# A two-layer transformer block on one core: all operations put in a new order, with other engines for 40 of them

## The chip, the cores and the metric

One core of a Trainium2 chip runs the whole program in one launch. The metric is the device time of that core in microseconds (us), the median of the runs.

## The reference

The input `x` is 2048 tokens of 512 features in bf16. Four residual blocks follow each other: attention, token MLP, attention, token MLP, with the same weights in both layers.

```python
def _A_ref(x, wqkv, wo):            # H = 32 heads of 16, window W = 256
    qkv = (x @ wqkv).reshape(B, S, 3, H, Dh).transpose(2, 0, 3, 1, 4)
    scores = einsum("bhqd,bhkd->bhqk", q, k) * (Dh ** -0.5)
    mask = (idx[:, None] - idx[None, :] >= 0) & (idx[:, None] - idx[None, :] < W)
    p = softmax(where(mask, scores, -1e9))
    return einsum("bhqk,bhkd->bhqd", p, v) ... @ wo
def _B_ref(x, w1, b1, w2, b2):      # mixes over the 2048 tokens, F = 1792
    u = gelu(einsum("bsd,sf->bdf", layernorm(x), w1) + b1)
    return (einsum("bdf,fs->bds", u, w2) + b2).transpose(0, 2, 1)
x = x + _A_ref(layernorm(x), ...);  x = x + _B_ref(layernorm(x), ...)   # twice
```

## The kernel before

The kernel first describes its work as a graph of 2440 operations, and only then gives every engine its queue. An operation is a short run of instructions on one engine: two matmuls of 512 columns, one eviction, one mask, one transfer. It knows what it reads and writes, and some operations have a second engine that can do them (`alts`). The string `ORDER` (lines 15 to 42), compressed, holds one order of all 2440 operations and for each the engine that is chosen; `begin_order` (line 44) unpacks it and `replay` (line 175) walks through it once. As it goes it hands each operation to its engine's queue and gives its tiles their buffers: the eight PSUM banks, 7 probability tiles, 4 buffers for `w1`, and so on. `emit` (line 196) then works out which semaphores each operation waits for. Every engine runs its queue strictly in order, so the string fixes who stands behind whom on each engine, which buffer is used again after what, and with it when each transfer may start. No time is in the string.

The work of one layer:

- Normalisation: statistics (line 492) and aggregation (494) on VectorE, the power -0.5 on GpSimd (505), the normalised rows on VectorE (512). In the first tokens of each layer TensorE transposes them (570, evicted at 577 or 579), elsewhere a DMA does (563).
- Projections, 128 columns at a time: K, Q and V operations on TensorE through the helper at line 534; evictions of Q at 592 (VectorE) or 594 (ScalarE), of K at 614 or 616, of V at 649 or 651. K is spread into a block-diagonal tile `kbd` by one of three ways: eight DMAs (624), or two instructions on GpSimd or VectorE (both line 629).
- Attention: 76 score blocks a layer, 152 in all, here numbered 1 to 152 in the order in which TensorE meets them; the order of scores is the same in both strings. A score block (710, some with bias matmuls at 721) fills four banks, ScalarE takes two exponentials from them (736), GpSimd masks the result (757), and TensorE forms the weighted sums (774). In the first eight blocks of 64 queries these come as 64 matmuls and 64 weight loads an operation. Behind a group of scores stand, in turn, a transpose (794) and a reciprocal (798) on VectorE, a product (800) on GpSimd or VectorE, a second transpose on VectorE (805), and the output projection W on TensorE with its residual (816).
- Token MLP: a first part U of `w1` is accumulated already during the attention (evicted at 880, 882 or 884), the rest L (895) behind it, then an addition (906) on VectorE and the gelu on ScalarE (910); the second product Y (534) with its residual (936). Y of the first layer runs into the second layer's attention. Weights come by 128 KB transfers on SyncE's queue (830 and 842).

Between two scores the order puts about three dense operations (K, Q, V, W, U or Y, two matmuls each), so that TensorE works while ScalarE takes its exponentials.

Of the kernel before, what the change touches and what calls it, by code (L numbers as in the profile page):

```python
# [14 lines left out]
ORDER = (
    'c-p;IA&l$T6@5<LtlqS5E3foc@=E@aw=!@gw{j(~WMJTxyp>ln2uP~{Z)K250RaI90R{mEUMV0TAi%&NARr*XARr(hARr)MfI&b&KvV^!(trU0z0PDZG'
    'yl)uzq{)8{y&cW{N8={o_p?j=Ia9EYe}!&L?lJXYD57>h99@89fUDLp4X6kUl)BtcN|Bvzq7yl24gnw>EBc;?T`h*e!p}DhuPnGE8AYJ>?NDc-EU{JnQ'
    'J?<nJLSPGG|{)lB7yQMUn<-s^rO^wmT_FllgSHMyo7)=X^gB#doRt=XP6FyItG%ZO?`+R26o09>x<(6iusP_r={V77bOCO-)l(#u(3gZN@4UCbX31K~Y'
    'YpHNRo}@kqenZGLz6@UYz)#yfp|x8T?7wXO>bO%SFNVItfMN6Pd2j$$dw=3p3G-2P&<Y=g}gb4}CuEaQ3KR}^J1i1i*=oI^m0jRpykB*?Pc5`=D#Qkrx'
    'kzUzmb(QTUTJuml~KQvpz;jkIhr$Jx`RI0aYLEzVtR?wHE?mso@FZD*F(R5v1g*<O-UX8#F{M2gO?QUDEZE}IE8FM@zHW~>6t5j=MjnGaE0V$RhT9nXk'  # L20
    'w`-V&VR_!x6GdIuD-|+xMbF=7WV>}-*Cn@r1DLLlM&uo(13?r;ScW=0>-0J#jvpv*nNdV1lL^n-`_H#@x7lotBtPCC<2c?Q_J@^ux3R2^Y38Q0PWSu$z'
    'qdPQV4CI%Kmk-I<1r*VG^eu^wlvLdk`B|9F@=f!fgtoDu+K(Gk_2rL3ry+ts4NJOej|)Jov_ge^1N}Uv;sxJg;lFHr&fjfGRrs|7}GSY+~qlyWqG+eMX'
    '_GBbbUHC3@po1Ivz_<?P|5^7p40uf(rnoS&ce#-Fn+zg{EnthG7&Ak?vL;86i#t7qAr|Bgw!|G0P;GW*CDvwgH}sqSWo`Xe{tNY};%$Wu;!1Wr_$91c5'
    '^ga^e|P7|-}@f*2Ht@>SOr1bXm0l*d@6r_%{s7Yhh%O}GtsqPznIpleOwm&<Iym_S*Yf|DxiLEX38eR6|ibT%#(@6t3yBd`=o=ZBP`F1!G*3?qt~jYP4'
    'kgt)RULyJiWqa>-zYnVdn7<s;fTnJdD$Z{(Xu;Chp;~Fl)dZH(TfvsyQa_WYupjy*|*K)0fR8<2`nt?hN5Tu%UIz_`_C5@s%y#uV_J3$Z(0&Lrr3P!}R'
    'N4Bi5okqQ0Z%Fc9SF2k6Un;oJG=-AMVllVAow6MnO#9$&EWQIcTCLWXj5QiRemRN&0^uvxG6QJ2dZR8$;Hb_sCd+8IlPjoNMHQa^f}eho*+5MD*0Kn2D'
    'XCN{EnQb(vg>ve57%lAkN`Wji?L;UI*5j7Xoju;eeey``u-l@Km}w09XEKtPvKS(@Amt}av|YD?;y8ioF>U4fk62VA90;dM^<EwwlG#y#mi29)sN$}dH'
    'he*+v^7K!uK^?m;HbIy&$e6N0JkU4~}CTpyRf?{qA&{O_y0VnqW4}*=D;L4gq16VmzH<oK5X4gG8XkXX8m`nt}kKCgSgI?a_ENf_fq}91V}?2m#~WZim'
    'CLANG0<@TqH>F@P6wb&R=|>tafAvmF#V0|w3INEOM1U(>ejA!q5J6u<$u;sTsVqpEG++YUV(_KxdpWZ>7_vaETnHl02^)E0zz9-7VMnj(X8D@BtSh5@}'
    'F>6YCNLstdYElFUkNl_sEP;`i@_`YgX6jfr9^ZnoQd@{+$o2~EP<^CFbfa+{E1zD9mk4=HYUkd(c2r}XU!4t?6_K^52$tF5zDyZ+|gia^e_1)ocjG`z>'  # L30
    '@-*>0j~^sFZ`*ON(+ZFUUV|3QhgxaJqwh0j8?DwFl-jawWLw}K5C(;dpcRp6nU?LGPNs!TKm(ou;;%`8i@rb$&6cFYfldV2)f5R)fQJeYrQh!>P&7$yQ'
    'fm9YEAoOMY9Jx%{lh&JY6x6SQzHG5tgrw~fD>e%g<&|If~=0m(ReWIC(zj_jan@TEog%Vn=Qzlv_nEL4`9Yl6k1iw4PD0p7usKmsu!kqI!#hQBQ=V`aw'
    '2rd351J*zA*HF5Y$&Y96_fw4GxjbMpemru~v*_R9%1+wkD>!P}TV?QI&452OB3TA&^lIw88HXo)rCvJx6n#*wV1)_dQiL;3QIUo@0cmD9gH%0W*2F90?'
    '*C7AFb_5n*w3x{XQ5aYqQ$q9Bh56l&;zkfY*>5|ZacV6_mVX58=jy(NlKG>GEy#0G(Kp=X0ut5&UsehZ^EvVtaRG#i#v#kK?TRkbX>@M@TrYT1#BR7nM'
    ';!$ejrCPD*?Vl3)uYViW9uT}z#RCPG}RZjw486rN<^*e#bD@aA4bdG1D7>0PYI2^M5@^BbGOeQllo{WQ>F<SH$%kSZM1ZsqFFP_LyKY*&Af&kN0KJ*PE'
    '3?u3{+x~n$M`(!`i{_+g<~oKZu2wQQj0TM~brQoik!iG>aLBs`)Z8!tHIo`xLb5DM5IOp}_W4_bpMCV<**K1a3;JcoT^4ZXmE742hsx#i*bP_wme1oi*'
    'DcOtW$wBYei|yQ7$}u~YR4k_#|bwVub+sp1paPbq<HiAP`dmPL`wJ^#nS{*y2QYt3nb^fN>_03`IGlL|7vCQ_CvY+VOZt2f#hCzyxv^~xtAl5RjIfXae'
    'd4ni4uCl?N1e%d)}GDPa}^oaKDrs*Erq+;NvlWlmMkSAbX1L0?{*tAL-0}!0>B^k4w%Fa$Na?$*;QN?cU%%3gB;SfB1FFKEHC0!j-;+mA;1g{Qvi;^aA'
    'qIxhlow=KXp+*6XowuR!F^tl?gh_z6?YJyzj58*{H||Ev#>-B~W*UfSt(qurt><tP{b&bKgj_EWwLl;3YjRQ?GHmP({_&bNf#7Nk<?b?#4~6_?VJc3ep'
    'IDSaxwC(n9v{;=e(gZMQH_!*D#HJh7q!CiC#;L`&Bh{Xr(SjKOO#``JbYduOY^DmWN-EgIgdOX#={HYU!<31Frw+F5*{6fusMISs<@}&>%g@#-;g?s<~'  # L40
    'OMQHNd>npS#c|KeUZ(aUo&TXiaL>W~Tn+jtA%8<PdrLX5U|tT`r%#AiHF@vn=LPuxP~iUpKz>0O'
)
# [973 lines left out]
```

## Time and profile before

| what | value |
|---|---|
| runs, median of 3 (lowest to highest) | 447.27 us (446.93 to 448.69) |
| profiled execution, span first to last instruction | 443.6 us |
| median of the runs less the span | 3.67 us |
| granted TensorE clock | 1.000 |
| busy: TensorE / VectorE / ScalarE / GpSimd | 96% / 70% / 72% / 47% |
| transferred | 45.01 MB in 98,736 packets |

The profile gives the profiled execution's time as its span alone; what lies around it (start and end of the launch) is the third row. The busy share of TensorE counts pipelined matmuls whose ends are modelled, so 96% does not say that it runs at its peak; how far apart the matmuls stand tells that. A wait that the profile puts down to "issue" is one that no semaphore, engine or transfer of the profile accounts for.

### The profile page before, as it was taken

To read this page: it belongs to the slowest core of one execution; us is meant where nothing else is said; L and a number is where in the kernel's file an instruction comes from. 1 tells how busy PE (TensorE), PEld (TensorE's weight loads), DVE (VectorE), ACT (ScalarE), POOL (GpSimd) and SP (SyncE) were. 2 spreads that over 40 slices of the span, in tenths; PEclk is the share of its full clock that TensorE was granted. 3 is DMA by queue.
4 is the path that set the end of the run, shared out by engine and by line. 5 is a ranking of instruction groups with operands and counts; after the bars stand their busy time and mean duration, and the time that the engine had idled before them with its cause. 6 is when DMAs were issued, how large, how long until landed. Compare 5 with 4: busy or idle time off the path is not lost.

```text
span 443.6 us, 14593 instructions
## 1 busy us (share of the span) xinstructions
PE 426.4 (96%) x6344; PEld 193.6 (44%) x6344; DVE 308.7 (70%) x573; ACT 317.4 (72%) x362; POOL 207.9 (47%) x316
## 2 busy tenths in 40 slices
PE   7898989999999999999999999999999999999996
PEld 6453444444433444444444444443344444444452
DVE  7997778778896579564787777789988456521134
ACT  3998999999999941726989899999999870440000
POOL 3486445746486531011566687968867751000000
PEclk9999999999999999999999999999999999999999
DMA  8574522301143446632255322131130447763533
GB/s 244 161 127 73 105 66 47 84 16 30 46 106 92 133 117 185 183 89 71 63 100 154 89 40 57 45 94 23 34 93 15 111 125 197 210 182 102 149 94 106
DMA packets 98736, 45.01 MB, mean 101 GB/s; under 512 B 28912, under 2 KB 98672, under 8 KB 98672
## 3 DMA queue, kind: packets, MB, share of 16 engines
q1 hardware_dynamic: 98672, 44.07, 39.1%
q8 instruction: 50, 0.82, 0.8%
q14 instruction: 14, 0.11, 0.1%
HBM read 33.56 MB, written 2.10 MB: 80 GB/s over the span
## 4 chain that ended last, share of the span: by engine, by line
PE 80%; ACT 12%; DVE 6%; issue 1%; POOL 0%; POOLq 0%
PE PS L534 54%; ACT pt L736 12%; PE PS L710 9%; PE PS L895 8%; PE PS L774 8%; DVE kbd L603 1%; DVE stats L492 1%; DVE xh_sb L512 1%; PE PS L721 1%; DVE rl L794 1%; DVE bb L472 0%; DVE qT L592 0%; DVE stg L614 0%; PE PS L570 0%; DVE vst L649 0%
## 5 line engine op out<-in xcount | busy, mean ns | idle before, releaser
L736 ACT ACTIVATE pt<-PS 128x1024 bf16<-128x1024 f32 (+1 forms) x304 | 281.7, 1036 | 16.0 <-PE PS L710 12.2
L757 POOL TENSOR_TENSOR pt<-pt,ldm 128x256 int32<-128x256 int32 (+2 forms) x226 | 145.1, 668 | 81.6 <-ACT pt L736 79.1
L534 PE MATMUL PS<-xh_sb,w1b 128*128 128x512 bf16 x280 | 68.9, 381 | 0.4 <-ACT pt L736 0.2
L534 PE MATMUL PS<-uT,w2b 128*128 128x512 bf16 (+1 forms) x294 | 69.1, 369 | 0.0
L534 PE MATMUL PS<-xhT,wqkv 128*128 128x512 bf16 (+1 forms) x288 | 67.0, 357 | 2.0 <-issue 0.6
L710 PE MATMUL PS<-qT,kbd 32*128 32x256 bf16 (+4 forms) x1488 | 60.2, 251 | 4.3 <-ACT pt L736 2.1
L505 POOL TENSOR_TENSOR rstd<-agg,mhalf 128x2 f32<-128x2 f32 (+1 forms) x33 | 22.8, 693 | 73.3 <-DVE agg L494 73.3
L936 DVE SCALAR_TENSOR_TENSOR x_sb<-PS,b2col,x_sb 128x512 bf16<-128x512 f32 x31 | 22.9, 746 | 46.6 <-PE PS L534 46.5
L794 DVE STREAM_TRANSPOSE rl<-PS 128x1024 f32<-128x1024 f32 x32 | 39.7, 1242 | 13.8 <-PE PS L774 13.3
L710 PEld LDWEIGHTS PS<-qT,kbd 32*128 32x128 bf16 x1488 | 21.6, 92 | 62.5 <-ACT pt L736 43.4
L910 ACT ACTIVATE uT<-rl,b1col 128x512 bf16<-128x512 f32 x28 | 18.5, 713 | 40.1 <-DVE rl L906 40.1
L774 PE MATMUL PS<-pt,vb 64*17 64x320 bf16 (+4 forms) x2976 | 43.5, 252 | 3.8 <-issue 1.9
L492 DVE BATCH_NORM_STATS2 stats<-x_sb 128x6 f32<-128x512 bf16 x64 | 43.1, 682 | 1.0
L534 PE MATMUL PS<-uT,pt 128*128 128x512 bf16 x168 | 41.2, 379 | 0.0
L534 PEld LDWEIGHTS PS<-uT,w2b 128*128 128x128 bf16 x294 | 27.2, 98 | 31.2 <-issue 3.2
L774 PEld LDWEIGHTS PS<-pt,vb 64*17 64x17 bf16 x2976 | 31.2, 84 | 19.1 <-issue 9.2
L534 PEld LDWEIGHTS PS<-xh_sb,w1b 128*128 128x128 bf16 x280 | 23.7, 98 | 31.8 <-issue 6.2
L895 PE MATMUL PS<-xh_sb,w1b 128*128 128x512 bf16 x168 | 37.4, 379 | 0.0
L534 PEld LDWEIGHTS PS<-xhT,wqkv 128*128 128x128 bf16 x288 | 23.9, 97 | 28.9 <-issue 5.5
L534 PE MATMUL PS<-wqkv,xhT 128*128 128x512 bf16 x128 | 33.9, 381 | 0.5 <-ACT pt L736 0.3
L534 PE MATMUL PS<-wo_sb,oT 128*128 128x512 bf16 x128 | 32.5, 380 | 0.2 <-DVE oT L805 0.2
L512 DVE TENSOR_SCALAR xh_sb<-x_sb,agg,rstd 128x512 bf16<-128x512 bf16 x64 | 29.7, 484 | 2.7 <-POOL rstd L505 2.5
(64 smaller groups left out, 339.8 us busy)
## 6 DMA issues: line engine op xcount, KB each, us to landing
w1b<-in_B_w_dram SPq DMA_DIRECT2D x112, 128.0 KB, 2.8
w2b<-in_B_w_dram SPq DMA_DIRECT2D x70, 128.0 KB, 2.8
pt<-in_B_w_dram SPq DMA_DIRECT2D x42, 128.0 KB, 2.8
vb<-vst SPq DMA_DIRECT2D x64, 68.0 KB, 2.1
out_dram<-x_sb SPq DMA_DIRECT2D x15, 128.0 KB, 2.0
x_sb<-in_A_x_dram SPq DMA_DIRECT2D x3, 512.0 KB, 7.5
wqkv<-in_A_wqkv_dram SPq DMA_DIRECT2D x4, 256.0 KB, 3.8
kbd<-stg SPq DMA_DIRECT2D x48, 16.0 KB, 1.9
```

The lines of the kernel that those rows point to most:

```text
L492: op("vector:stat", lambda e: e.bn_stats(st[:, 0:6], x_sb[:, t, :]), reads=[f"x{t}"], writes=[("st", i)], cost=dve_cost(512))
L505: op("gpsimd:rstd", lambda e: e.tensor_tensor(rstd[:, t0:t1, 0], agg[:, t0:t1, 1], mhalf[:, 0:1].to_broadcast([P, t1 - t0]), op=ALU.pow), ...
L512: op("vector:xh", lambda e: e.tensor_scalar(xh_sb[:, t, :], x_sb[:, t, :], agg[:, t, 0:1], rstd[:, t, :], op0=ALU.subtract, op1=ALU.mult), ...
L534: return e.matmul(o, lhsT=w, rhs=x, start=start, stop=stop, skip_group_check=True)
L710: last = e.matmul(bank(tt[r // 2], r % 2)[:, base + c0 * 64:base + (c0 + n) * 64], lhsT=kbd[32 * r:32 * r + 32, tk.slot, o, jj].rearrange( ...
L736: op("scalar:exp", lambda e, ts=ts, tp=tp, i=i, cols=cols: e.activation(probs(tp)[:, i, 0:cols, :], pair(ts)[:, :, 0:cols].rearrange("p r ...
L757: return e.tensor_tensor(v, v, m, op=ALU.mult)
L774: last = e.matmul(bank(t, h)[32 * r:32 * r + 17, i + q0 * 64:i + (q0 + n) * 64], lhsT=vb[64 * h:64 * h + 64, tk.slot, jj, 4 * o + r, :], r ...
L794: op("vector:od", lambda e, t=tod, tr=tr: e.transpose(rl[:, tr.slot:tr.slot + 2].rearrange("p a b -> p (a b)"), pair(t)), reads=[(tod, i) ...
L895: last = e.matmul(bank(tu, tt), lhsT=v()[:, sc - b0, k0 + tt * P:k0 + (tt + 1) * P], rhs=xh_sb[:, sc, :], start=(sc == b0), stop=(sc == NT ...
L910: op("scalar:gelu", lambda e, ft=ft, tt=tt: e.activation(uT[:, ft, :], rl[:, tmps[tt].slot], ACTF.Gelu_apprx_tanh, bias=b1col[:, ft:ft + 1 ...
L936: op("vector:resy", lambda e: e.scalar_tensor_tensor(x_sb[:, t, :], bank(ft), b2col[:, t:t + 1], x_sb[:, t, :], op0=ALU.add, op1=ALU.add), ...
```

## The change

Only the string `ORDER` is replaced. The graph, the operations, the buffers and the code that gives out queues and semaphores stay.

```diff
 ORDER = (
-    'c-p;IA&l$T6@5<LtlqS5E3foc@=E@aw=!@gw{j(~WMJTxyp>ln2uP~{Z)K250RaI90R{mEUMV0TAi%&NARr*XARr(hARr)MfI&b&KvV^!(trU0z0PDZG'
...
+    'c-p;HKZx_l6(4zLzti5$7bY-;K9~!0puiNmpaTUI(18Lf6i^|84jgdd!Urx~xX^(L6)IG?Foy~k3aD_QfD02`nBc;N3kO`daIuApEnIA|#THv^v4x9_*WO+4'
...
 )
```

Unpacked, the two strings compare like this. All five queues differ, most operations by a few places: on average an operation moves 4.6 places of 922 on TensorE, 4.4 on VectorE, 3.1 on ScalarE, 3.3 on GpSimd and 10.3 on SyncE. The sequence of the 152 scores is untouched. Of the operations that may run on either of several engines, 40 change:

| operations | from | to | how many |
|---|---|---|---|
| Q, K, U, V evictions, transposed rows | VectorE | ScalarE | 15 |
| Q, K, V evictions | ScalarE | VectorE | 6 |
| K spread (629, 624) | GpSimd | VectorE | 6 |
| K spread | DMA | VectorE / GpSimd | 2 / 2 |
| product (800) | GpSimd | VectorE | 6 |
| product | VectorE | GpSimd | 2 |
| the ones of `vst` (479) | VectorE | GpSimd | 1 |

Operations on each queue, before and after: TensorE 922 and 922; VectorE 559 and 561; ScalarE 359 and 368; GpSimd 299 and 292; SyncE 301 and 297. K spreads on GpSimd, DMA, VectorE: 13, 6, 5 before and 9, 2, 13 after. Products on GpSimd and VectorE: 18 and 14 before, 14 and 18 after.

TensorE's queue between scores, where it matters here (P is one weighted-sum operation, T a transpose of rows, the number behind a letter how many stand together):

```
behind score   before                          after
 3 ..  6       V4 | Q T2 | Q K | K V2 K        V Q V | V2 T2 | - | K Q K V2 K
13, 14         P2 | V2                         P | V2 P
17, 18         Q3 | Q P2                       Q P Q2 | Q P
37 .. 40       U2 | P2 | U2 | U3               U3 | U P2 | U3 | U3
48, 49         P2 | U2                         P | P
60, 61         U2 W2 | W3                      U2 W2 | W3
76 (to the second layer's first score)
   before   U7 P2 U8 W2 U W6 U7 L26 Y L Y L Y27 T Y2 V2 Y T Y2 V Y V T2 Y3 K2 Y2 Q2 V2
   after    U7 P2 U8 W4 U2 W2 U W U4 W U L22 Y L5 Y3 L Y30 T Y3 T Y2 T2 V Y3 K2 V Q4
77 .. 80       Q2 Y2 | V2 Y2 K | K3 Y2 | Y3    V2 K V | V3 K3 | Y4 | Y3
128, 129       V4 | P2                         V3 | V P2
147 .. 149     U4 | U2 P2 | U3                 U3 | U3 P2 | U3
152 (to the end)
   before   U8 P2 U2 L3 W6 L W2 L31 Y L7 Y118
   after    U7 P2 U L2 U L W8 L39 Y119
```

On VectorE, the operation of line 512 that stood between the K eviction behind the 59th score and the V eviction that follows it is moved behind the next U eviction. On ScalarE, evictions among the exponentials: a Q eviction more behind the 17th score; between the 78th and the 104th score eight where there were five; three U evictions behind the 148th and 150th scores where there were none, and four behind the last score where there were three.

More of the change, by code (lines that the diff above doesn't have):

```diff
@@ L20 @@
[L20 to L24, printed above, removed]
@@ new lines @@
+    'NVc*z7gx)rZQEqE`f@g-o6U?;v>FcifYR~k?(U8nMQON*e0lM;b<<dPEWE%=X9dwLoN9=Vo17!WSnl--R;v{`8+g1d*>cJ3@O|9YvQTV@`f(kFjD=AUgsre$'
+    'mjA9V@Th3F+et!`s7Pp0q!H~kBfshgxY=lUp55>Wvn;<FRI61LU0q#Y-QCqLYZ$k#WABm}OV6p{>GYd_jSO=bcu3bBr;09vC~|ja!lu#fqK=_h3gbLjuXRIT'
+    'a!#pfo0flZVL8syS+3A~GSdksh!<QHCs)g&$TCEfZLfz>#~TpkdUG||B%9m2+h+6bE_+|=tk>7K7_G*e%|()&uk6*#j?BWIPUot6bv2)_*K2Q>=l1z>B&XKg'
+    'DyRL~yx;HJqp?r^Zjx_F+3)wVtoP?$-ox0o`(-~>Rof^i<(RQv7KT|Cwma9?##N_f7`!dZ?W!Eqo6V-Gaxd@!cT|~DS=Togx=zl|?Un7?OUKb<O`D9@OKwg$'
@@ new lines @@
+    '?qil?Sx)`T_iKsZPm=VbJa==KQf6B`HlsMHitSt~JG!h9g`8o_rj#1mnrfOxu!7Gf>dus*pyxPd;&??bw|cg!&;-S?5ow{JzsFe9G4C}pzhS5}U?O*xYML_R'
+    '8dE5vf`XLl(`koLQ*e|6?M|uHY8uyded}y3Sw7SC1u$>c*Yh==&mq(h!o$<S_U>*7Zjp>Jl7)3rC=5s-ALRKKH=ENe&+`%3&7?8_zQ3WWtI8m5M2;{Bk^ngl'
+    'u$o#GL7@4_b2+yR1^@)8FvHAj119Rkvcv#&b;cFWn8J346i_Hu$1|92=?jbMq~kh{m{1W|VJu$GCON?XqtwsUIE&-Bu4z#fQ4JHMAm5K7U*KTbwp9fHdjbMV'
+    'm&;26=ks%@Y4&(V`NSIIdn>*ITkt_fc^F1#XR_REbUFyir@DR`*6Xz(2&&)LzpmFcSckGqF?3zzpPtDO%!F+@EEl#lzj2)5(CO6DG_BRTjYit&h(c>Sx^8M7'
@@ new lines @@
+    'htT&_)3FTz08v#!bO0e&i6l#g$OIN%rb*E4?d>%}NM9@#=bMcHSJj7;;dwe9t0PSt2wV$I^RnFc7(36h)k-OUTmGZk{ZU~GpbE0JQ?=wWjO%rs>)%n4GNv*Y'
+    'Lc6t+<;M3LzFfBX`U0>1fEJ6AfmuFSET@ZtF)%La7=UrJ2}bqls8$1kBfBekI9yD1IoC9)>}SFOj}XB)>-O&;>=#KQb)_uIFt)O!i_H<nol=i1p%7CTg;_Q0'
+    'R<c$%%i19boodag1MYfGvs(2;O5JL;&W8hs*K0x|8jS5K%drEYKECS%lQ^cR_49K_t6C6ZHqrg*G`PGBdIcD(*Ur_|KQ->yg7K=U8pdW5U)WKkYjLcGmTQS3'
+    'Y1ok+;?~ubt{M98&jG)^k^R43se(cm4O(9<mkUbgA|q{8`Jnu6P>x0;H*hDO=eW~yOrW#SEK!i<e7-39L=mLw!SPO_I-R2YvUibQ;=EVIdEmO^F&=l_K~|=e'
@@ L42 @@
+    'bfD5bxCdgtqSS$<(lL^vBq4lMf)nuKcBdR?JN?*~)QMQU7n*xzd8uE*Pd))}7s|6Lsys)ca#U=)%kF!xr=L}h)>Xg(5a}&q+)q5kBos$H?67(Fv}!-Q`;*?i'
+    '+YRmp#1DcOT67PCw8u#Vzencu<mBxV1g|EghtpR+0?6y9O64)ehj1$|rMB|AmmHKtdaH`0=jsOzJbAGkNXJ?wN&i#HNv}mvdXQO3l3o&VuO5;FB<WZM_JdD)'
+    '@^Ie6*zxGW@v-~8Ao)*pub+?PztWmVG5>#5{FgB4r{5%j2gDxiS@nEeiho_z{SPfNNM8'
 )
```

30 lines of the change are left out of this document (10 added, 20 removed).

## The prediction

> **What bounds the kernel now.** I read the page's busy line first, then the table by stage, then the chain that ended last, then who ScalarE waited for.
>
> ```profile
> span 443.6 us, 14593 instructions
> PE 426.4 (96%) x6344; PEld 193.6 (44%) x6344; DVE 308.7 (70%) x573; ACT 317.4 (72%) x362; POOL 207.9 (47%) x316
> 10.00:42.00 32.00, 27.35 (x648) 15.90 (x648) 27.79 (x68) 29.62 (x38) 20.04 (x25) 1.00 0.61 131
> ...
> 57.00:118.00 61.00, 56.96 (x1277) 25.80 (x1267) 47.83 (x83) 60.12 (x65) 32.94 (x51) 1.00 0.20 43
> 118.00:157.00 39.00, 38.48 (x687) 15.67 (x686) 29.25 (x54) 37.40 (x42) 25.83 (x40) 1.00 0.38 101
> 157.00:205.00 48.00, 48.00 (x325) 22.05 (x324) 31.89 (x60) 17.42 (x25) 5.76 (x9) 1.00 0.51 141
> 205.00:281.00 76.00, 75.95 (x1155) 31.72 (x1154) 58.48 (x103) 68.49 (x78) 48.70 (x74) 1.00 0.35 81
> 281.00:357.00 76.00, 75.24 (x1357) 31.02 (x1355) 60.75 (x103) 72.57 (x78) 58.71 (x89) 1.00 0.26 64
> 357.00:443.60 86.60, 82.94 (x498) 38.89 (x496) 32.78 (x56) 15.21 (x22) 5.73 (x9) 1.00 0.51 145
> ```
>
> The columns are the stretch, its length, and the busy time of TensorE, its weight loads, VectorE, ScalarE and GpSimd. The first attention (10 to 157) is filled on ScalarE: from 57 to 118 it works 60.12 of 61 us. The second (205 to 357) is filled on TensorE, 151.2 of 152 us, with ScalarE close behind at 141.1. The token-MLP stretches (157 to 205, 357 to the end) are TensorE alone. The median of the runs, 447.27, is 3.67 us above this span; I carry that unchanged, so a microsecond of span is a microsecond of time.
>
> ```profile
> 34.87 1.39 issue
> 46.15 0.54 issue
> 66.38 25.79 ACT pt L736 x28
> 289.59 1.83 PE PS L534 x8
> 291.43 0.33 PE PS L710 x8
> 291.76 1.40 PE PS L534 x6
> 293.16 0.33 PE PS L710 x8
> 294.46 1.33 PE PS L774 x91
> 391.99 47.96 PE PS L534 x236
> ```
>
> These are pieces of the chain in order of time. In the dense tail a matmul takes 47.96/236 = 0.203 us. Between two scores TensorE needs 0.33 for the score block and 1.40 for three dense operations (six matmuls), together 1.73; ScalarE needs two exponentials of 25.79/28 = 0.921, together 1.84. So the two engines are nearly balanced. The new order has the same 152 scores, the same 304 exponentials and all the same matmuls, so none of this sum moves. Only the idle time in it can.
>
> ```profile
> ACT pt L736 <- PE PS L710: 3.3, 4, 1.7
> ACT pt L736 <- PE PS L721: 2.2, 6, 1.1
> ACT pt L736 <- PE PS L710: 8.9, 17, 1.1
> ```
>
> The first two rows are the waits of the exponentials for scores in the first attention, 5.5 us, and the third those in the second, 8.9 us. The first 5.5 us are on the path; the 8.9 lie where TensorE is full and mostly cost nothing.
>
> **The change part by part.** *Two weighted-sum pairs pulled apart.* The longest waits of ScalarE in the first attention are these:
>
> ```profile
> 33.67 1.20 PE L774 MATMUL PS<-pt,vb 64*17 64x64 bf16 x101 [0.35 <-DVE stats L488]
> 36.26 0.57 PE L774 MATMUL PS<-pt,vb 64*17 64x192 bf16 x27 [1.39 <-issue]
> 37.22 1.02 ACT L736 ACTIVATE pt<-PS 128x1024 bf16<-128x1024 f32 x1 [1.74 <-PE PS L710]
> 47.55 1.02 ACT L736 ACTIVATE pt<-PS 128x1024 bf16<-128x1024 f32 x1 [1.05 <-PE PS L721]
> q8 instruction: 50, 0.82, 0.8%
> q8 instruction: 1, 0.02, 2.3%
> ```
>
> TensorE stops after 101 of 128 matmuls and waits 1.39 us for nothing that the profile shows except the queue of instructions. That queue moved 0.82 MB in 50 packets over the span, 16.4 KB each, against 12,688 matmuls and weight loads: about 254 instructions a packet. The last row is the stretch from 32.5 to 37: one packet, 2.3% of 16 engines in 4.5 us, or 1.66 us. A pair of these weighted sums is 128 matmuls and 128 loads, a whole packet's worth, wanted in some 1.3 us; before has both pairs back to back, behind the 13th and behind the 18th score, and both show in the chain (1.39 and 0.54). After has one half behind the 13th, then a score, two V operations and the other half; and one half among the Q operations behind the 17th, the other behind the 18th. The same 256 instructions then span at least one more score interval, 1.84, so some 2.4 or more against the 1.20 + 1.39 = 2.59 that the first one took. Between 0 and 0.2 us of stall is left, and ScalarE has an exponential queued to cover it. The two waits together are 2.79; I take 2.5 as gained, with 0 and 2.8 as ends (0 if the stall only moves to the next pair).
>
> The Trainium skill, "Runtime: NRT & Kernel Launch", section "Instruction fetch mechanics", speaks against this: refills come in 16 KiB blocks of 256 instructions, and crossing a block's border is mostly hidden. The block size agrees with 254 a packet; the 1.39 us does not agree with hidden. By that rule this term would be nothing.
>
> *A normalisation moved out of GpSimd's way.* Behind the 60th score TensorE loses about half a microsecond:
>
> ```profile
> 124.00 0.94 DVE L512 TENSOR_SCALAR xh_sb<-x_sb,agg,rstd 128x512 bf16<-128x512 bf16 x1
> 124.15 0.40 PE L710 MATMUL PS<-qT,kbd 32*128 32x320 bf16 x8
> 125.71 1.02 PE L534 MATMUL PS<-wo_sb,oT 128*128 128x512 bf16 x4 [0.20 <-DVE oT L805]
> 126.79 0.40 PE L710 MATMUL PS<-qT,kbd 32*128 32x64 bf16 x12
> L512 DVE TENSOR_SCALAR xh_sb<-x_sb,agg,rstd 128x512 bf16<-128x512 bf16 x64 | 29.7, 484 | 2.7 <-POOL rstd L505 2.5
> ```
>
> From score to score 2.64, where four dense operations take 1.83 + 0.33 = 2.16. The line-512 operation took 0.94 against a mean of 0.484, and the transpose and the V eviction behind it came late. After puts this operation behind the U eviction that follows; late next is the residual of W (816), which a bank waits for. Gain 0.45, ends -0.5 and 0.5.
>
> *One dense operation leaves the tail.* Behind the last score before has 179 dense operations, after 178; the other went into the second attention, among intervals that wait for ScalarE. Gain two matmuls, 0.4 us (ends 0 and 0.4).
> ```profile
> 18.30 1.09 ACT L736 ACTIVATE pt<-PS 128x512 bf16<-128x512 f32 x2 [0.32 <-PE PS L710]
> ```
>
> *The start* changes by reordering alone. This wait of ScalarE stands behind the transposes that follow the 4th score; after puts two V operations ahead of those and a score right behind them. Gain 0.3, ends -0.5 and 0.5.
>
> *Nine more evictions on ScalarE.* From 359 operations to 368.
>
> ```profile
> L592 DVE CAST qT<-PS 128x512 bf16<-128x512 f32 (+1 forms) x32 | 20.1, 632 | 10.5 <-PE PS L534 10.5
> L594 ACT CAST qT<-PS 128x512 bf16<-128x512 f32 x2 | 1.2, 614 | 0.0
> 344.21 7.56 ACT L736 ACTIVATE pt<-PS 128x1024 bf16<-128x1024 f32 x8 [0.73 <-PE PS L710]
> 352.47 4.92 ACT L736 ACTIVATE pt<-PS 128x1024 bf16<-128x1024 f32 x5 [0.70 <-PE PS L710]
> ```
>
> One new Q eviction, 0.614, stands behind the 17th score, where ScalarE is full: +0.5 on the path. Three of U, at about the same length 1.8 us, stand behind the 148th to 150th scores, where ScalarE idles 0.73 + 0.70 = 1.43: +0.4. Three more than before stand between the 78th and 104th scores, inside the 8.9 us of waits above: 0. The remaining two stand outside the attentions: 0. Without that cover all seven in the attentions would cost 7 x 0.61 = 4.3.
>
> *Work moved to VectorE.* Spreading K (line 629) goes from 5 to 13 operations on VectorE, of two instructions each; it leaves GpSimd (13 to 9) and the DMA queue (6 to 2, so 32 of 48 transfers of 16 KB go, and the transposes behind them on the queue come sooner; no wait of TensorE in the trace names a transfer). The products of line 800 go from 14 to 18 on VectorE.
>
> ```profile
> L800 DVE TENSOR_TENSOR ul<-rl,rc 128x512 bf16<-128x512 f32 x14 | 10.4, 744 | 0.3
> 250.02 0.57 DVE L629 TENSOR_SCALAR kbd<-stg,par 128x512 bf16<-128x512 bf16 x2
> 282.42 1.43 DVE L629 TENSOR_SCALAR kbd<-stg,par 128x512 bf16<-128x512 bf16 x2
> ```
>
> A spread took 0.57 with GpSimd quiet and 1.43 with masks running. Eight more are 4.6 to 11.4 us and four products 3.0, against nine evictions that leave, 9 x 0.632 = 5.7: VectorE gains 1.9 to 8.7 us of work in 443, and is 70% busy. Behind it on the queue stand evictions that free TensorE's banks. I take 0, because VectorE waits for TensorE in most rows of its evictions (10.5 in the Q row alone); the end is 6.9 (the stretched part, 8 x 0.86) + 3.0 = 9.9 if all of it is exposed.
>
> The sum: -2.5 - 0.45 - 0.4 - 0.3 + 0.5 + 0.4 = -2.75. 447.27 - 2.75 = 444.5 us.
>
> **The rivals.** *VectorE is held and becomes late* (slower). The moved spreads meet masks, each stretched to 1.43, and the evictions behind them keep banks from the next score. For it: 124.00 above, one stretched operation, cost TensorE 0.48 us. Against: VectorE's share, and an order that takes line 512 out of the one place where its stretch shows. It decides once over a quarter of the 9.9 is exposed (2.75); at two thirds the time is 444.5 + 6.6 = 451.1. "GPSIMD Engine Reference" of the Trainium skill, section "Key points", says that GpSimd shares its SBUF interfaces with VectorE and names contention with two-input and two-port instructions; the 0.57 against 1.43 agrees, and the rule is against this part of the change.
>
> *The issue stall stays* (no change). If the pause belongs to any burst of weighted sums, or moves to another pair, the 2.5 is not gained: 447.0. For it: other pairs stand together in both orders. Against: the pair at 294.46, of 2 x 56 matmuls, runs through in 1.33 without a pause.
>
> *More idle goes than I can name* (faster). All 5.5 us of the exponentials' waits in the first attention, 0.4 in the tail: 447.27 - 5.9 = 441.4; with a quarter of the 8.9 besides, 439.2.
>
> **How the numbers follow.** Forecast 0.56, held VectorE 0.17, stall stays 0.19, more idle goes 0.08. Half a per cent, 2.24 us, is about what a measurement of this kernel can tell from no change. The forecast is 0.5 from that line, so 0.12 of its 0.56 counts as no change: faster 0.44 + 0.08 = 0.52; same 0.12 + 0.15 = 0.27 (the rest of the stall's case, 0.04, goes to slower, with unpaid evictions of up to 4.3); slower 0.17 + 0.04 = 0.21. The range runs from 439.5, nearly all of the last rival, to 451.5, just past two thirds of the first; about a tenth is left out on each side.
>
> **What would show it.** Right: no issue row over 0.5 us at the weighted sums between 30 and 48; ScalarE's waits for scores in the first attention at 3 us or less; the score behind the 60th after about 2.16 us; ScalarE's tail stretches as busy as before. Wrong: rows in which TensorE or the exponentials wait for line 629 or line 800 on VectorE, most spreads of line 629 on VectorE near 1.43 rather than 0.57, or new issue rows at the split pairs.

## The result, and the profile after

The changed kernel takes 443.82 us (median of four runs, 443.62 to 445.56) against 447.53 for the kernel before beside it (four runs, 446.93 to 448.69): a ratio of 0.992, with a 95% interval of 0.9897 to 0.9942. A second comparison, in the first experiment below, gave 0.9952. So the change gains between half a per cent and one. The forecast was 444.5.

The profiled execution of after happens to be the slowest of the four, 445.56 us with a span of 443.6; the spans of the other three are 441.7 to 441.9. The opposite holds for before: its profiled span of 443.6 belongs to one of its short executions, since its runs in the comparisons below lie 1.7 us above their own spans (1.68 to 1.80), which puts that one near 445.3, under all four times above. Equal spans in the two pages therefore do not mean equal kernels.

From the page of after, the busy line and one of the costliest groups (the last columns are busy time and mean, then the idle time before them and what ended it):

```profile
span 443.6 us, 14491 instructions
PE 418.5 (94%) x6270; PEld 193.5 (44%) x6344; DVE 307.4 (69%) x582; ACT 322.7 (73%) x372; POOL 201.1 (45%) x305
L512 DVE TENSOR_SCALAR xh_sb<-x_sb,agg,rstd 128x512 bf16<-128x512 bf16 x64 | 27.2, 445 | 3.2 <-POOL rstd L505 3.1
```

TensorE has 6270 matmul records where 6344 were issued: 74 are missing from this trace. They, and not a change, make its busy time smaller, and they leave small holes of 0.16 us that the profile calls issue.

The table by stage of after (columns as in the prediction: stretch, length, TensorE, weight loads, VectorE, ScalarE, GpSimd, then granted clock, DMA share and GB/s):

```profile
5.00:10.00 5.00, 3.26 (x22) 2.09 (x20) 4.01 (x14) 2.01 (x4) 1.02 (x2) 0.76 0.99 302
205.00:281.00 76.00, 74.50 (x1143) 31.66 (x1156) 54.70 (x97) 71.63 (x85) 46.32 (x71) 1.00 0.35 84
281.00:357.00 76.00, 72.91 (x1340) 31.11 (x1354) 61.28 (x111) 73.19 (x81) 54.28 (x82) 1.00 0.23 56
357.00:443.60 86.60, 82.92 (x491) 39.11 (x500) 32.67 (x56) 16.91 (x24) 5.68 (x9) 1.00 0.51 145
```

ScalarE has more in each stretch of the second attention (71.63 where it had 68.49). With a granted clock of 0.76 between 5 and 10 us, the first exponential of this execution comes at 10.80 (table below), where two kernels with the same start at full clock have 9.55 and 9.57; that is most of the 1.7 to 1.9 us by which it is longer than the other three.

Who waited, in after: the exponentials in the first attention (10 to 157; first two rows), in the second (205 to 357; third), and TensorE's weight loads for the spread of K on VectorE (last):

```profile
ACT pt L736 <- PE PS L721: 2.7, 9, 0.6
ACT pt L736 <- PE PS L710: 1.7, 4, 1.0
ACT pt L736 <- PE PS L710: 6.3, 14, 0.7
PEld PS L710 <- DVE kbd L629: 0.7, 2, 0.4
```

The waits for scores fell from 5.5 to 4.4 and from 8.9 to 6.3; nobody waits to speak of for the spreads that moved.

Where the time goes is best seen between landmarks. This table takes the start of the first exponential of the 1st, 13th, 19th, 57th, 77th, 109th and 152nd score from each trace (row by row, us); "first" counts from the first instruction that does work, 0.31 us behind the start of the span. It already has the kernels of the experiments.

| kernel | first | 1-13 | 13-19 | 19-57 | 57-77 | 77-109 | 109-152 | 152-end |
|---|---|---|---|---|---|---|---|---|
| before | 10.46 | 22.74 | 14.04 | 71.44 | 87.34 | 67.67 | 84.20 | 85.42 |
| before again | 11.67 | 22.37 | 14.08 | 71.69 | 87.78 | 67.81 | 84.20 | 85.41 |
| before, pairs split | 10.46 | 23.02 | 14.65 | 71.39 | 87.57 | 67.79 | 84.40 | 85.41 |
| before, new start | 9.58 | 22.54 | 13.43 | 71.58 | 87.49 | 67.83 | 84.23 | 85.41 |
| before, 42 more at the start | 10.73 | 23.11 | 12.45 | 74.69 | 87.33 | 67.55 | 84.57 | 85.42 |
| before, 25 more at the start | 10.48 | 24.65 | 12.05 | 74.05 | 87.43 | 67.55 | 84.24 | 85.62 |
| before, new start and 25 more | 9.90 | 22.74 | 12.03 | 72.59 | 87.56 | 67.73 | 84.22 | 85.41 |
| after | 10.80 | 22.77 | 12.99 | 72.18 | 88.01 | 66.96 | 85.21 | 84.39 |
| after again | 10.53 | 22.90 | 12.70 | 72.31 | 87.50 | 66.98 | 85.17 | 84.38 |
| after, pairs joined | 9.55 | 22.74 | 12.81 | 72.64 | 87.69 | 66.96 | 85.23 | 84.39 |
| after, Q back on VectorE | 9.57 | 22.62 | 12.63 | 72.93 | 87.79 | 66.98 | 85.16 | 84.38 |
| after, 54 more at the start | 12.29 | 22.30 | 13.43 | 72.93 | 87.78 | 66.99 | 85.53 | 84.38 |
| before's order, after's engines | 11.89 | 23.57 | 13.92 | 73.77 | 88.46 | 68.90 | 87.47 | 85.23 |
| after's order, before's engines | 12.31 | 22.79 | 12.65 | 72.65 | 88.96 | 69.85 | 92.98 | 85.54 |

Before against "after, pairs joined", both at full clock throughout, reads: start -0.91, 13th to 19th -1.23, 19th to 57th +1.20, 57th to 77th +0.35, 77th to 109th -0.71, 109th to 152nd +1.03, behind the last score -1.03; together -1.3 us. Hardly any of these is where the prediction looked for it at the size it gave.

### The profile page after: what moved, and what is told of

Its sections match the earlier page's. It is cut to its first block, busy times and chain, and to the rows that moved or that the text cites. A ratio compares the mean times of both kernels' runs of the same rounds, so it can differ in the third digit from the quotient of the medians.

```text
span 443.6 us, 14491 instructions
## 1 busy us (share of the span) xinstructions
PE 418.5 (94%) x6270; PEld 193.5 (44%) x6344; DVE 307.4 (69%) x582; ACT 322.7 (73%) x372; POOL 201.1 (45%) x305
## 4 chain that ended last, share of the span: by engine, by line
PE 79%; ACT 13%; DVE 3%; issue 2%; DMA 1%; SPq 1%; POOL 1%; POOLq 0%
PE PS L534 53%; ACT pt L736 12%; PE PS L710 9%; PE PS L895 8%; PE PS L774 8%; DMA w1b<-in_B_w_dram 1%; DVE rl L794 1%; PE PS L721 1%; DVE stats L492 1%; SPq L830 1%; PE PS L570 0%; DVE vst L649 0%; DVE bb L472 0%; DVE x_sb L816 0%; POOL rstd L505 0%
## 5 line engine op out<-in xcount | busy, mean ns | idle before, releaser
L757 POOL TENSOR_TENSOR pt<-pt,ldm 128x256 int32<-128x256 int32 (+2 forms) x226 | 146.9, 675 | 91.7 <-ACT pt L736 91.2
L534 PE MATMUL PS<-xhT,wqkv 128*128 128x512 bf16 (+1 forms) x267 | 65.3, 362 | 4.5 <-issue 1.4
L534 PE MATMUL PS<-xh_sb,w1b 128*128 128x512 bf16 x262 | 66.0, 380 | 2.9 <-issue 1.9
L534 PE MATMUL PS<-uT,w2b 128*128 128x512 bf16 (+1 forms) x285 | 66.7, 370 | 0.8 <-issue 0.5
L534 PE MATMUL PS<-uT,pt 128*128 128x512 bf16 x163 | 39.5, 380 | 0.3
L895 PE MATMUL PS<-xh_sb,w1b 128*128 128x512 bf16 x164 | 37.0, 379 | 0.7 <-DMA w1b<-in_B_w_dram 0.6
L534 PE MATMUL PS<-wqkv,xhT 128*128 128x512 bf16 x115 | 32.3, 381 | 3.5 <-issue 1.3
L512 DVE TENSOR_SCALAR xh_sb<-x_sb,agg,rstd 128x512 bf16<-128x512 bf16 x64 | 27.2, 445 | 3.2 <-POOL rstd L505 3.1
```

Of the source, the lines that this page charges most:

```text
L512: op("vector:xh", lambda e: e.tensor_scalar(xh_sb[:, t, :], x_sb[:, t, :], agg[:, t, 0:1], rstd[:, t, :], op0=ALU.subtract, op1=ALU.mult), ...
L534: return e.matmul(o, lhsT=w, rhs=x, start=start, stop=stop, skip_group_check=True)
L757: return e.tensor_tensor(v, v, m, op=ALU.mult)
L895: last = e.matmul(bank(tu, tt), lhsT=v()[:, sc - b0, k0 + tt * P:k0 + (tt + 1) * P], rhs=xh_sb[:, sc, :], start=(sc == b0), stop=(sc == NT ...
```

## The experiments

The first four share one set of runs of before: both kernels again, the split of the pairs made alone, and the packets of TensorE's instructions moved.

**Both kernels again.** No edit.

> The kernel before, run once more, for what lies around its span. The profile of before has a span of 443.6 us and its runs a median of 447.5; that of after has the same span of 443.6 in a run of 445.56, the others of after have spans of 441.7 to 441.9 in runs of 443.6 to 443.8, so 1.9 around the span. If 1.9 holds for before too, its usual span is 445.5 and the profiled one was a short one by 2 us; then every theory expects spans near 445.5 here and a time of 447.3, ratio 1.000. If before has 3.7 around its span, the spans are 443.6.

> The kernel after, run once more, for a profile at full clock from the start (the first one had 0.88 in the first 10 us) and a narrower interval. Expected: ratio 0.992, span 441.8, no issue row over 0.5 us at the weighted sums between 30 and 48 us, the exponentials' waits for scores in the first attention at 4.4 us or less (5.5 before).

Before again: 447.01 us (445.44 to 448.15, 12 runs), ratio 1.0004 [0.9988, 1.0021]. After again: 444.3 (444.05 to 444.95, 6 runs), ratio 0.9952 [0.9934, 0.997] to a before of 446.52 (445.12 to 448.04, 29 runs). Before spreads over 3 us, after over less than 1. The pauses of before are there again, but with other lengths. Its timeline of TensorE, at the 13th and the 18th score:

```profile
34.50 1.19 PE L772 MATMUL PS<-pt,vb 64*17 64x64 bf16 x101 [0.35 <-issue]
36.58 0.57 PE L772 MATMUL PS<-pt,vb 64*17 64x192 bf16 x27 [0.89 <-issue]
...
45.03 1.48 PE L772 MATMUL PS<-pt,vb 64*17 64x64 bf16 x120
47.55 0.30 PE L772 MATMUL PS<-pt,vb 64*17 64x256 bf16 x8 [1.03 <-issue]
```

They stand at the same matmul as in the first trace of before (behind the 101st of the first pair), now 0.89 and 1.03 where the first trace had 1.39 and 0.54. (Line numbers in these kernels are two lower than in the kernel before: 772 is the weighted sum, 734 the exponential, 708 the score, 510 the normalisation, 568 the transpose, 627 the spread, 532 the dense helper; in the kernels with more matmuls at the start they are one higher, 775, 737, 711 and so on.)

**The split alone.** The pairs of the 13th and 18th score are pulled apart in before's order. On VectorE the transpose (794) that reads the moved half's result goes behind two normalised rows (512); all else is as before.

```diff
 behind score
-13, 14   P2 | V2          17, 18   Q3 | Q P2
+13, 14   P | V2 P         17, 18   Q2 P Q | Q P
```

> The kernel before with one part of the change alone: the second weighted sum behind the 13th score moved behind the two V operations of the 14th, and one of those behind the 18th moved in front of the second Q behind the 17th. All else as before. If the prediction's first term holds alone, both pauses go and the time falls by 2.5 us to 444.8 (ratio 0.9945). If pulling apart only moves the work (the half pair behind the 14th and 17th scores makes those intervals longer by 0.8), half of it is given back: ratio 0.997. If the gain of after lies elsewhere: 1.000.

446.86 us (445.89 to 449.3, 12 runs), ratio 1.0017 [1.0, 1.0034]: no gain. The prediction had -2.5 for this. TensorE around both places:

```profile
33.94 0.85 PE L772 MATMUL PS<-pt,vb 64*17 64x64 bf16 x64 [0.35 <-issue]
36.77 0.47 PE L772 MATMUL PS<-pt,vb 64*17 64x64 bf16 x33
38.97 0.40 PE L708 MATMUL PS<-qT,kbd 32*128 32x256 bf16 x8 [1.36 <-DVE rl L792]
44.05 0.84 PE L772 MATMUL PS<-pt,vb 64*17 64x64 bf16 x64
46.22 0.73 PE L772 MATMUL PS<-pt,vb 64*17 64x64 bf16 x56
47.56 0.30 PE L772 MATMUL PS<-pt,vb 64*17 64x256 bf16 x8 [0.60 <-issue]
```

The pause at the 13th is gone, and 13th to 14th takes 1.81 instead of 3.71; but 14th to 15th takes 3.93 instead of 1.82. Only part of that is the moved half: the 15th score waits 1.36 us for VectorE's transpose of the moved half's result (row at 38.97), a wait that after does not have, where the V eviction stands ahead of that transpose. So this run does not price the pause alone. Behind the 18th a pause stays although only one half stands there. From the 13th to the 19th it takes 14.65, where before took 14.04.

**The packets moved.** 42 small matmuls more ahead of the 42 of the warm-up (84 instructions with their weight loads, so that every border between packets of 256 falls 84 instructions earlier in the work behind); the order is before's.

```diff
+            for _ in range(42):
+                e.matmul(PS[:, warm.slot, 0:64], lhsT=uT[0:32, 0, 0:P], rhs=uT[0:32, 0, 0:64], start=True, stop=True,
+                         tile_position=(0, 0), skip_group_check=True)
```

> The kernel before, unchanged in order and engines, with 42 small matmuls (32 x 128 weights, 64 columns) more at the head of the warm-up, where TensorE waits for data anyway: 84 instructions more, so every border of an instruction packet falls 84 instructions earlier in the work. Packet theory: the pauses of 1.39 and 0.54 us belong to a packet whose 256 instructions are wanted faster than the next can be had; shifted by 84, no packet of the early attention holds a whole pair of weighted sums, both issue rows go, the exponentials' waits in the first attention fall by 1.5 to 2.5 us, and the time falls to 445 to 446 (ratio 0.995). Burst theory (any pair of weighted sums pauses, wherever the borders are): both rows stay, ratio 1.000, or a little over for the extra matmuls.

446.58 us (445.24 to 449.2, 12 runs), ratio 1.0007 [0.9989, 1.0025]. Both pauses are gone, 13th to 19th takes 12.45, and the time is the same, because a new one stands behind the 48th score (and one of 0.47 behind the 8th). TensorE there:

```profile
102.57 0.31 PE L722 MATMUL PS<-bb,sel 32*128 32x96 bf16 x12
104.63 0.22 PE L722 MATMUL PS<-bb,sel 32*128 32x96 bf16 x4 [1.75 <-issue]
106.49 1.89 PE L535 MATMUL PS<-wo_sb,oT 128*128 128x512 bf16 x4
```

The table by stage around it (granted clock third from the right):

```profile
103.00:106.00 3.00, 1.21 (x12) 0.43 (x14) 1.66 (x4) 1.10 (x2) 0.00 (x0) 1.00 0.14 23
106.00:110.00 4.00, 4.00 (x43) 1.41 (x44) 2.04 (x4) 2.74 (x4) 2.95 (x5) 0.57 0.22 49
```

It stops in the middle of the bias matmuls of a score for 1.75 us; and then the granted clock drops to 0.57 for 4 us, in which four dense matmuls take 1.89 us where six took 1.47. 49th to 53rd takes 8.66 against 7.24. One pause is paid twice.

The next four: the same in after, and order and engines apart.

**The pairs joined in after.** Only TensorE's queue changes, in these places.

```diff
 behind score
-13, 14   P | V2 P         17, 18   Q P Q2 | Q P
+13, 14   P2 | V2          17, 18   Q3 | Q P2
```

> The kernel after with one part undone: the weighted sums behind the 13th and 14th, and behind the 17th and 18th scores stand together again as before. If the pulling apart is the main term (2.5 us): ratio to before 0.9975. If half of it is given back where the halves land: 0.9945. If it is worth nothing in this order: 0.992 as after.

444.28 us (444.09 to 445.09, 7 runs), ratio 0.9946 [0.9925, 0.9967]: as after. The two pairs run through, or nearly. TensorE:

```profile
32.83 1.86 PE L772 MATMUL PS<-pt,vb 64*17 64x64 bf16 x128 [0.38 <-POOL rstd L503]
43.30 1.53 PE L772 MATMUL PS<-pt,vb 64*17 64x64 bf16 x128
```

128 matmuls in 1.86 and 1.53 us, in the very arrangement that paused in before. It is not the arrangement of the pair. Nor is it the place of the packets' borders: the pairs stand within six instructions of where they stood in before, counted from the start of TensorE's queue, so the borders fall at the same places in them. At the first border TensorE has a hole of 0.36 us between two starts (33.76 to 34.12), at the second none. What differs in the traces is when the packet comes. Its transfer began 0.4 and 0.9 us ahead of TensorE's reaching the border before (at 31.57 and 41.54); in before it began 0.45 behind and 0.16 ahead of it (33.24 and 43.69), in before again 0.22 and 0.18 behind. What makes it begin sooner was not found.

**The packets moved in after.** 54 more matmuls at the start (108 instructions).

> The kernel after with 54 small matmuls more at the head of the warm-up: 108 instructions more, so every border of an instruction packet falls 108 instructions earlier in the work. By TensorE's own work between borders (each operation at its shortest length in the profile of before), the shortest packet of after lasts 2.3 us without and 3.0 us with this shift. Packet theory: what is left of pauses goes, 0.3 to 1 us under after, ratio to before 0.990 to 0.991. Burst theory: as after, 0.992.

446.96 us (446.17 to 448.77, 12 runs), ratio 1.0003 [0.9985, 1.002]: the whole gain is gone. Two parts show. The added matmuls take 3.06 us at the start and the first exponential comes at 12.29 (after: 10.80 and 10.53); and pauses are back, one of them inside a half pair that stands alone. TensorE:

```profile
35.14 0.59 PE L775 MATMUL PS<-pt,vb 64*17 64x64 bf16 x46 [0.38 <-POOL rstd L506]
36.23 0.48 PE L775 MATMUL PS<-pt,vb 64*17 64x192 bf16 x18 [0.51 <-issue]
...
40.27 1.25 PE L535 MATMUL PS<-xhT,wqkv 128*128 128x512 bf16 x5 [0.89 <-issue]
```

13th to 19th takes 13.43 against 12.70 to 12.99. The delay of the start is the larger part, so this run alone does not price the pauses.

**Engines without the order, order without the engines.** Before's order with after's choice for all 40 operations, and after's order with before's choice.

> The order of before, with the 40 engine choices of after. If the gain lies in who does what (GpSimd relieved, ScalarE with nine evictions more, 32 transfers of 16 KB fewer), ratio 0.992 to 0.996. If engines are worth nothing by themselves, or harm where the order was not made for them: 1.000 to 1.006, with exponentials waiting longer than the 5.5 us of before in the first attention.

> The order of after, with the engine choices of before. If the order alone makes the gain: ratio 0.992 to 0.994. If order and engines only work together: 0.997 to 1.003. If the engines make it: 1.000.

455.44 us (454.66 to 455.64, 5 runs), ratio 1.0187 [1.0162, 1.0213], and 459.87 (459.47 to 460.14, 6 runs), ratio 1.0288 [1.0263, 1.0313]. Each half alone costs 8.5 and 12.9 us; together they gain. The exponentials' waits for scores, first of old order with new engines (first attention, two rows; second attention), then of new order with old engines (second attention):

```profile
ACT pt L734 <- PE PS L719: 4.5, 9, 1.3
ACT pt L734 <- PE PS L708: 3.4, 6, 1.2
ACT pt L734 <- PE PS L708: 9.8, 19, 1.0
```

```profile
ACT pt L734 <- PE PS L708: 18.9, 26, 4.3
```

One place of new order with old engines shows the mechanism, in the timelines of GpSimd, TensorE and ScalarE:

```profile
280.40 1.36 POOL L627 TENSOR_SCALAR kbd<-stg,par 128x512 bf16<-128x512 bf16 x2 [1.70 <-DVE stg L612]
281.73 2.79 POOL L755 TENSOR_TENSOR pt<-pt,ldm 128x256 int32<-128x256 int32 x4
283.19 0.65 PE L772 MATMUL PS<-pt,vb 64*17 64x64 bf16 x40 [2.03 <-POOL pt L755]
284.22 1.02 ACT L734 ACTIVATE pt<-PS 128x1024 bf16<-128x1024 f32 x1 [2.72 <-PE PS L708]
```

A spread given back to GpSimd waits 1.70 for the K eviction and runs 1.36; the masks queue behind it, the weighted sum waits 2.03 for the masks, and the next exponential waits 2.72 for its score. In after that spread is VectorE's, takes 0.60 there, and no mask stands behind it. So a price for one such move, with the order kept, is no price for it in the new order.

The last four: the start, and one eviction.

**The new start alone.** Before, with the 63 operations ahead of the first score in after's order and on after's engines (both copies of the transposed rows on ScalarE, the first Q eviction on VectorE, the ones of the V tile on GpSimd).

```diff
 VectorE, first microseconds
-masks x3, reduce, mask, memset, mask, reduce, mask, statistics, memset, copy, aggregate, statistics, aggregate, reduce, normalise
+memsets, masks x5, reduce, statistics, aggregate, statistics, aggregate, normalise
```

> The kernel before with the start of after alone: the 63 operations that stand in front of the first score in after are taken in the order of after and with its engines (both first transposed rows evicted on ScalarE, the first Q on VectorE, the ones of vst on GpSimd), all else in the order of before. In the profiles at full clock the first exponential starts at 9.85 us with the start of after and at 10.77 with that of before. Start theory: the first exponential 0.9 to 1.1 us sooner, nothing lost behind it, ratio to before 0.9975 to 0.998. If ScalarE or a transfer takes the gain back within the first attention: 1.000.

445.4 us (444.11 to 446.24, 12 runs), ratio 0.9959 [0.9943, 0.9975] to a before of 447.2 (445.17 to 449.27, 29 runs): 1.8 us, most of what the whole change brings. Statistics, first transposes and first exponential, of before and then of this kernel:

```profile
3.91 0.69 DVE L492 BATCH_NORM_STATS2 stats<-x_sb 128x6 f32<-128x512 bf16 x1
6.34 0.48 PE L570 MATMUL PS<-ident,xh_sb 128*128 128x128 bf16 x4 [0.58 <-DVE xh_sb L512]
10.77 2.45 ACT L736 ACTIVATE pt<-PS 128x1024 bf16<-128x1024 f32 x3
```

```profile
3.25 0.68 DVE L490 BATCH_NORM_STATS2 stats<-x_sb 128x6 f32<-128x512 bf16 x1
5.67 0.61 PE L568 MATMUL PS<-ident,xh_sb 128*128 128x128 bf16 x4
9.89 1.94 ACT L734 ACTIVATE pt<-PS 128x1024 bf16<-128x1024 f32 x2
```

One mask and one reduction fewer stand ahead of the statistics, and a memset, a copy and a reduction fewer between them and the normalised rows, so the statistics begin 0.66 us earlier, the transposes 0.67 and the first exponential 0.88. In this execution TensorE no longer idles between warm-up and transposes. That idle time can matter beyond its own length: in before again it was longer, and the clock fell. The transposes there:

```profile
6.33 0.40 PE L568 MATMUL PS<-ident,xh_sb 128*128 128x128 bf16 x4 [1.23 <-DVE xh_sb L510]
```

The stretch from 5 to 10 us, of before again and then of this kernel:

```profile
5.00:10.00 5.00, 2.47 (x18) 1.53 (x17) 4.24 (x18) 1.04 (x3) 1.12 (x2) 0.77 1.05 325
```

```profile
5.00:10.00 5.00, 3.91 (x44) 2.81 (x42) 4.69 (x17) 2.85 (x7) 1.03 (x2) 1.00 1.03 314
```

Clock 0.77, and the first exponential at 11.97 instead of 10.77. The length of the idle time alone does not decide: 0.58 us left the clock at 1.00 in before, and 0.43 us was followed by 0.79 in after again.

**The packets moved by 25, in before and behind the new start.** 25 small matmuls at the start (50 instructions).

> The kernel before with 25 small matmuls more at the head of the warm-up: borders of instruction packets 50 instructions earlier in the work. By TensorE's own work between borders, the tightest packets of before are 1.44 us (13th score) and 1.84 us (18th); with the 84 instructions of the earlier run 1.81 us at the 49th, where that run did pause for 1.75; with 50 the tightest is 2.66 us. Packet theory: no pause over 0.4 us at the weighted sums, 1.2 to 1.8 us gained of the pauses of 1.1 to 1.6 and 0.8 to 1.3, ratio 0.996 to 0.997, and runs closer together than those of before (445.1 to 448.6). Against it: pauses near the 13th and 18th scores as before, ratio 1.000.

> Both of these together: the start of after and the shift of 50 instructions, on the order and engines of before. If start and pauses are the whole gain of after, ratio to before 0.994 to 0.995, as after (0.9952 and 0.992). If a third part is needed (the reordering elsewhere, the other engines), 0.997 or more.

448.9 us (446.02 to 450.92, 12 runs), ratio 1.0036 [1.0015, 1.0057]; and 446.75 (444.21 to 448.14, 12 runs), ratio 0.998 [0.9959, 1.0001], against 0.9959 [0.9943, 0.9975] for the new start without it. What is left of the expectation that a chosen number of instructions clears the pauses is the place that it was chosen for: 13th to 19th takes 12.05 and 12.03, the shortest of all, with both pairs together. Elsewhere they came up. TensorE in before with 25 more, behind the 8th and behind the 24th score:

```profile
27.82 0.23 PE L711 MATMUL PS<-qT,kbd 32*128 32x128 bf16 x4 [2.13 <-issue]
58.13 0.46 PE L775 MATMUL PS<-pt,vb 64*17 64x320 bf16 x14 [0.83 <-issue]
60.19 0.93 PE L535 MATMUL PS<-xhT,wqkv 128*128 128x512 bf16 x3 [1.27 <-DVE rl L795]
```

The table by stage behind the second:

```profile
60.00:64.00 4.00, 3.81 (x36) 1.62 (x38) 2.84 (x7) 2.85 (x4) 2.83 (x4) 0.59 0.00 0
```

2.13 us in the middle of a score block; then 0.83, a wait of 1.27 for VectorE right behind it, and the clock at 0.59 for 4 us. 1st to 13th takes 24.65 against 22.74, and 19th to 57th 74.05 against 71.44. Behind the new start, with the work in the packets shifted alike, the pause behind the 8th score was 0.28 and the one behind the 24th 0.83. By its expectation a ratio of 0.997 or more asks for a third part of the gain; since the shift brings 0.83 us of its own, this run does not show one. The first pair runs through; TensorE:

```profile
33.14 1.52 PE L775 MATMUL PS<-pt,vb 64*17 64x64 bf16 x128 [0.37 <-issue]
```

That profiled execution is again a short one (444.21); its other runs are up to 4 us longer.

**The Q eviction behind the 17th score back on VectorE**, in after.

> The kernel after with one engine choice undone: the Q eviction behind the 17th score back from ScalarE to VectorE. The prediction put 0.5 us on it. In the profiles the stretch from the 19th to the 57th score is 0.6 to 1.2 us longer in after than in before. If this eviction is the reason: 0.3 to 0.6 us under after, ratio to before 0.0010 lower than after in the same call would have, about 0.994. If VectorE is late with it: 0.5 us and more over after.

444.2 us (443.71 to 444.71, 6 runs), ratio 0.9929 [0.9907, 0.9951], which can't be told from after. 17th to 19th takes 4.44 against 4.51 and 4.80, so this eviction cost at most 0.1 to 0.4 us there (the joined kernel, which has it on ScalarE, took 4.28); 19th to 57th is no shorter (72.93), so it isn't what makes that stretch longer in after. No kernel that was run is clearly below after.

**Where the pauses stand**, counted in the traces. Five traces have every instruction of TensorE (before, before again, the split, 42 more, after again). Behind the start, the issue rows of 0.4 us or more in them stand behind 1217 and 1730 instructions (before, both traces), 1730 (the split), 707 and 4289 (42 more) and 3010 (after again). Divided by 256 each leaves 193 to 195, so each stands at a border between packets, and each ends 1.3 to 2.2 us behind the end of a packet's transfer (in before at 36.26, the transfer at 34.88). Of 245 borders, TensorE reached seven less than 2.7 us behind the one before; all seven paused, by 0.47 to 1.75 us. Of the other 238 one paused by 0.47 and the rest by 0.25 at most. A late transfer does it too: the 2.13 us in before with 25 more came although the border was reached 3.4 us behind the last, because the transfer began only 3.3 us behind that one.

The border behind 3010 instructions, after the 34th score, is a pause that the new order has and before has not. TensorE in after again and in the kernel with Q back on VectorE:

```profile
76.19 0.39 PE L532 MATMUL PS<-wqkv,xhT 128*128 128x512 bf16 x1 [0.47 <-issue]
```

```profile
75.46 0.39 PE L532 MATMUL PS<-wqkv,xhT 128*128 128x512 bf16 x1 [0.98 <-issue]
```

It is 0.47 in after and 0.73 with the pairs joined; in before, before again and the split it is 0.25 at most.

## Why the prediction came out right

The total, the sign and the chances held; the steps behind them mostly did not. That the sum came within 0.7 us is in good part luck: it was made on the trace of a short execution, its largest term had the wrong cause, and gains and losses that it did not name nearly cancel.

- **The pairs pulled apart, -2.5: the step that failed.** The stretch it spoke of did gain, 14.04 to 12.99 and 12.70 (1.1 to 1.4 us), and no issue row above 0.5 us is left there in after. In the part it described the prediction is borne out: with the halves apart TensorE reaches the two borders 3.7 and 3.0 us behind the ones before them (after again), where before has 1.8 and 2.0. But that is not what the gain hangs on. Joined again in after, the pairs reach the same borders after 1.8 and 2.0 us, and neither the stretch (12.81) nor the time grows. Alone, the split gives 1.0017 [1.0, 1.0034]: its half behind the 18th score still paused by 0.60, with 2.6 us from border to border where the prediction took 2.4 to be about enough, and its half behind the 14th ran into a wait of 1.36 for VectorE. And 25 more matmuls at the start clear both pauses with the pairs together. The prediction saw that the pause belongs to a packet of instructions, and then took the burst to be the whole cause; the runs show that it is a border reached sooner than its packet, so that a later border or an earlier packet ends it. Why the packets come earlier in after's order is open. The pair at 294.46 that the prediction held against the rival (96 matmuls, not 2 x 56) has a border inside too, but TensorE reached it 7.6 us behind the last. The rival of no change, that the pause moves elsewhere, is what happened in before with 42 and with 25 more and in after with 54 more; in part it happened in after itself, behind the 34th score.
- **The page cited there.** By "Runtime: NRT & Kernel Launch", section "Instruction fetch mechanics", of the Trainium skill, crossing a border is mostly hidden, and the term would be nothing. "Mostly" agrees: the trace of before has some 50 borders and two pauses. The pauses of 0.5 to 2.13 us do not agree with "hidden". That the split alone brings nothing agrees, but for another reason, the waits that it brought.
- **The start, -0.3: a term mis-sized.** The new start gives 0.88 us between two executions at full clock and 1.8 us in the medians (not all of it need be the start: in its trace 13th to 19th is 0.6 shorter too), and not by the transposes behind the 4th score but by VectorE's set-up ahead of the first statistics. The rows at 3.91 and 6.34 stood in the trace of before. In the two traces of after itself the clock fell there (0.76 and 0.79), and the first exponential (10.80 and 10.53) came no sooner than in the first trace of before (10.46).
- **The normalisation behind the 60th score, -0.45: right, a little less.** The next score came 0.35 us sooner. In the timeline of TensorE of after:

```profile
124.26 0.40 PE L710 MATMUL PS<-qT,kbd 32*128 32x320 bf16 x8
124.59 1.04 PE L534 MATMUL PS<-xh_sb,w1b 128*128 128x512 bf16 x4
125.46 1.03 PE L534 MATMUL PS<-wo_sb,oT 128*128 128x512 bf16 x4
126.50 0.40 PE L710 MATMUL PS<-qT,kbd 32*128 32x64 bf16 x12
```

  2.24 from score to score where before had 2.64, close to the 2.16 forecast; the wait for `oT` is gone. The stretch from the 57th to the 77th as a whole is no shorter (87.50 and 88.01 against 87.34 and 87.78).
- **A dense operation out of the tail, -0.4: cancelled.** Behind the last score 1.03 us goes, and 109th to 152nd takes 1.03 more (85.23 against 84.20). What was moved or added there, the dense operation and the three U evictions, would account for it: the intervals were taken to have room. That was not tried by itself.
- **Nine evictions on ScalarE, +0.9.** The one behind the 17th cost at most 0.1 to 0.4 rather than 0.5. The three more between the 78th and the 104th score, taken at nothing, came with a gain: 77th to 109th fell by 0.7. That was not seen, and which edit brings it wasn't tried. Between the 19th and the 57th after loses 0.5 to 1.5 us (71.44 and 71.69 against 72.18 to 72.93), which the prediction had not seen either; 0.5 to 1.0 of it is the new pause behind the 34th score, and without that 71.7 to 72.0 are left (the kernel with 54 more has 72.93 without that pause, so it is not all).
- **Work to VectorE, 0: right.** The spreads on VectorE have a median of 346 ns, the weight loads waited 0.7 us for them in all, and line 512's mean fell from 484 to 445 ns. The rival of a held VectorE did not come. With the new engines in the old order the loss is 8.5 us, near its end of 9.9, but that loss wasn't traced to VectorE. One row of after, all operations of line 629 on VectorE (count: shortest/median/longest, ns):

```profile
L629 DVE TENSOR_SCALAR kbd<-stg,par x26: 253/346/917, 63.7 to 346.2; 128x512 bf16<-128x512 bf16 x26
```

- **What would show it.** Issue rows: held. The score behind the 60th: held. Waits for scores at 3 us or less in the first attention: missed, 4.4. The tail as busy on ScalarE: missed, 16.91 for 15.21.
- **3.67 us around the span: wrong.** It is 1.7 us for before's kernels and 1.9 to 2.0 for after's. 3.67 compared one short execution with the median of others, so nearly 2 us of before's usual time were not in the trace that the sum was made on; changing pauses and the clock are seen to differ between executions.

So the gain of 2.2 to 3.7 us has these parts: the start 0.9 to 1.8, shown by a run of its own; shorter pauses between the 13th and 19th score, 1.1 to 1.4, where it is shown that they stand at the borders but not what in the new order shortens them; the score behind the 60th, 0.35, and 77th to 109th, 0.7, seen in the traces alone; against these 0.5 to 1.5 lost between the 19th and the 57th, up to 1.0 of it by a new pause. The first two parts may overlap. Part of the difference of the medians is that before is seldom at its best. Open are what makes a pause 0.5 us in one execution and 1.4 in the next, how much of before's spread is pauses and how much clock (its runs at full clock are not clearly its fastest: beside the last four kernels they have a median of 447.64, 8 runs, where all 29 have 447.2), and what else the 19th to 57th loses.

## What to carry to other kernels

Before a stall is put down to the instructions that it stands in, move it: a few harmless instructions at the start shift all that follows, and a stall that jumps elsewhere belongs to the supply of instructions. Count the instructions ahead of it as well: stalls at the same remainder of one number are one cause. Price an edit of order and an edit of engines together, since each alone can cost several times what both gain. And take the first chain of a kernel (load, statistics, first transposes) as seriously as its long stages: a microsecond of set-up work ahead of it was a microsecond of the end time here, and an idle TensorE there can cost clock as well.
